# A new plan of work for a decode step: other heads first, fewer second-layer loads, one form of feed-forward

## The chip, the cores and the metric

The kernel runs on one core of a Trainium2 chip. The metric is the time of one execution on the device in microseconds. The core has a matrix engine (PE; its weight loads are shown as PEld), a vector engine (DVE), a scalar engine (ACT), GpSimd (POOL), a queue that issues transfers (SP), and 16 DMA engines that carry them. The engines run side by side, each through its own list of instructions in order, and wait for one another by semaphores.

## The reference

Four tokens (B = 4), one position each, go through attention, feed-forward, attention, feed-forward. The two attentions use the same weights and the same caches, and so do the two feed-forwards.

```python
x = A_x
x = x + _A_ref(_layernorm(x), A_k_cache, A_v_cache, A_wq, A_wo)
x = x + _B_ref(_layernorm(x), B_w_gate, B_w_up, B_w_down)
x = x + _A_ref(_layernorm(x), A_k_cache, A_v_cache, A_wq, A_wo)
x = x + _B_ref(_layernorm(x), B_w_gate, B_w_up, B_w_down)
```

`_A_ref` has 16 query heads on 8 key-value heads of 256 numbers each, and reads the last 2048 of 8192 cache positions: softmax of q.k / 16, times v, times `wo`. `_B_ref` is `(silu(x @ w_gate) * (x @ w_up)) @ w_down` with 1792 inner columns. x has 448 numbers for each token, and all is in bfloat16.

For each token and key-value head there is 1 MiB of keys and 1 MiB of values: 64 MiB for 32 pairs of token and head. The weights are small beside it.

## The kernel before, in words

**Heads and groups.** A unit of work is a head, written as three digits: token, layer (0 first, 1 second), key-value head. PLAN lists the stages in order; in a stage a blank separates groups, "+" joins two heads that share one group (one softmax for both), and "&" does the same with the score matmuls issued for each head apart (or, behind a single head, with the wide form of the scores). `group` (L859) makes the steps of one group: query spread over the array (`qe`, POOL), scores (`sc`, PE, L920), maximum, `spread`, `negm`, `exp`, `turn`, copy (`pt`), sum, the product with the values (`pv`, PE, L1001), and `oh`, `oho`, `flip`, `oT`, which lead to a column for the output projection `out_proj` (L1039). The keys of a half load are first transposed in place on DVE (L887), at one instruction for each half.

**Half loads and slots.** Keys and values are held in SBUF in slots of 512 KiB, one half load each: four for a head. NPOOL = 31 slots are in the pool. NLATE = 7 more lie where the query weights `wq` are, and can be used only after the last query projection. Keys named in WHOLE come as one transfer of two neighbouring slots, the others as two transfers. SLOTS gives the slot of each such transfer in the order of SP's list. A transfer into a slot that is taken waits for the last reader of what lay there: the score matmuls of a key, the `pv` of a value.

**Held halves.** A token's second layer reads the same caches as its first. What HOLD names (a key head counts as two halves, a value half as one) stays in its slot from the first layer to the second. What it does not name is loaded again: 128 half loads for the first layer, and 128 less the held ones for the second.

**The change of layer.** When all eight first-layer heads of a token are done, the stage loop (from L1068) appends: `rows` (the projections added up in row form are split, turned and added), the last output projection in column form (`opc`), `residual`, `norm`, the feed-forward, `norm` again and `qproj`, which gives the query of the second layer. Only after that can the scores of this token's second layer run, and give back what it holds. The feed-forward has two forms: `ffn_row` (L658) for the tokens in ROWF, with the token's hidden values in rows, after which `rows` and `residual` are run again, and `ffn` (L711), with them in columns, which adds straight into x. A token whose second layer is done waits, and its last feed-forward is run together with another token's.

**Order.** `Graph` collects the steps with what each reads and writes, and numbers them as they are made. The order on each engine is not found by the program: SEQ_PE, SEQ_DVE, SEQ_ACT, SEQ_POOL and SEQ_SP are written out, each a list of step numbers. SEQ_PE also has fillers, "w" and a number: a matmul of 512 columns on zeros into bank A (L1137 in the trace, and L543 where one follows another), which only keeps PE at work. The number says behind which reader of bank A it may run. Since SP issues in order, a transfer that waits for its slot holds back all later ones.

```python
if held[s] is not None:
    o.deps[last[id(held[s])]] = True
elif s >= NPOOL:
    o.deps.update((d, True) for d in late)
held[s] = cell
```

These lines of `schedule` give a transfer its slot and its wait.

**Lines.** L521 loads weights (`load`); L875 and L881 load keys, whole and by halves; L897 values; L740 and L776 are the two products of the column feed-forward, L678 and L706 those of the row form; L615 is the query projection; L654 copies the finished query; L812 adds the residual; L820 stores the result.

Of the kernel before, what the change touches and what calls it, by code (L numbers as in the profile page):

```python
# [37 lines left out]
ROWF = (1, 2)  # L38
PLAN = (
# [4 lines left out]
)  # L44
HOLD = (
# [3 lines left out]
)  # L49
WHOLE = (  # L50
    "000 001 002 003 004 005 006 007 010 011 012 014 015 017 100 101 102 103 104 106 107 110 112 202 203 204 206 "
    "211 215 216 300 301 302 303 304 307 314"
)
SEQ_PE = (
# [32 lines left out]
)  # L87
SEQ_DVE = (
# [256 lines left out]
def build(nc, A_x, A_k_cache, A_v_cache, A_wq, A_wo, B_x, B_w_gate, B_w_up, B_w_down, out):  # L345
# [3 lines left out]
    with ExitStack() as es:  # L349
# [718 lines left out]
        for si, (heads, splits) in enumerate(zip(plan(), plan_splits())):  # L1068
# [40 lines left out]
            for t, layer in full:  # L1109
                residual(t)  # L1110
                norm(t, xr)
                if layer == 0:
                    with_, waiting = waiting, []
                    if t in ROWF:
                        ffn_row(with_ + [t])
# [86 lines left out]
```

## Time and profile before

| what | value |
|---|---|
| median of three runs | 277.8 us (275.09, 281.72, 277.8) |
| span of the profiled execution | 277.7 us, from its first to its last instruction; this is the time to which the sums below refer |
| PE busy | 242.4 us, of which the fillers (L1137 and L543) 53.3 and 51.8 |
| DVE busy | 185.0 us |
| ACT and POOL busy | 62.8 and 80.4 us |
| bytes read | 100.77 MB |
| value transfers | 83 of 512 KiB |
| key transfers | 30 of 1024 KiB, 26 of 512 KiB |
| mean TensorE clock granted | 0.984 |

In the rows by stretches of time, each engine's busy time is given with its number of instructions in brackets; the three numbers at the end are the granted clock of PE, the busy share of the DMA engines, and GB/s. In rows in order of time, the first number is the start, the second the duration, then engine, line, operation, result and operands; what the engine waited for stands in square brackets. In rows by group, the busy time and the mean in ns come first, then the idle time of the engine ahead of the group and what ended it. The chain line gives shares of the span along the chain of work that ended last.

### The profile page before, as it was taken

Reading aid. Unit: us, or ns where it says so; the run is one execution under the profiler, and the core shown is the slowest. Engines: PE = TensorE matmul, PEld = TensorE weight load, DVE = VectorE, ACT = ScalarE, POOL = GpSimd, SP = SyncE. Lnnn points to the kernel's source line nnn. Section 1 sums busy time; section 2 is a strip of 40 time slices with the busy share of each in tenths; the row PEclk is TensorE's granted clock in tenths of the full one; section 3 lists DMA queues with packets and bytes.
Section 4 is the critical chain, followed back from the end, with each engine's and each line's share of the span. In section 5 each row is a group of like instructions: output and inputs, shape, how many; then the busy total and the mean of one; then the engine's idle time right before and its main releaser. Section 6 shows DMA issues by size and latency. Waiting matters only on the chain.

```text
span 277.7 us, 10576 instructions
## 1 busy us (share of the span) xinstructions
PE 242.4 (87%) x4751; PEld 126.5 (46%) x4576; DVE 185.0 (67%) x574; ACT 62.8 (23%) x173; POOL 80.4 (29%) x224
## 2 busy tenths in 40 slices
PE   3997999999999887998888887979799787989995
PEld 0121232233475553544445444535455456667664
DVE  4666817735612687978857599986768757389841
ACT  0003021111112222331332333224132321232411
POOL 1160121111024221615044243133234332254350
PEclk9998899999999999999999999999989999999998
DMA  7999999999999999999999999999999998799200
GB/s 278 425 420 413 415 395 418 399 401 406 405 387 417 411 412 414 410 409 411 351 394 400 414 417 411 408 413 408 358 384 350 411 378 297 279 396 411 81 2 3
DMA packets 25740, 101.44 MB, mean 365 GB/s; under 512 B 2523, under 2 KB 6623, under 8 KB 21471
## 3 DMA queue, kind: packets, MB, share of 16 engines
q1 hardware_dynamic: 25687, 100.78, 91.8%
q8 instruction: 36, 0.59, 0.9%
q14 instruction: 9, 0.07, 0.1%
q10 hardware_dynamic: 8, 0.00, 0.0%
HBM read 100.77 MB, written 0.00 MB: 363 GB/s over the span
## 4 chain that ended last, share of the span: by engine, by line
PE 40%; DMA 36%; DVE 14%; issue 3%; ACT 2%; SPq 2%; POOL 2%; DVEq 0%; ACTq 0%
DMA half<-in_A_v_cache_dram 24%; DMA half<-in_A_k_cache_dram 12%; DVE half L887 8%; PE S L920 8%; PE A L543 6%; PE Y L1001 6%; PE A L1137 5%; PE Z L740 3%; PE A L1055 2%; PE Z L776 2%; PE A L1047 1%; PE Y L969 1%; SPq L521 1%; DVE oh L1019 1%; SPq L897 1%
## 5 line engine op out<-in xcount | busy, mean ns | idle before, releaser
L887 DVE STREAM_TRANSPOSE half<-half 128x1024 uint32<-128x1024 uint32 x86 | 104.7, 1229 | 8.8 <-DMA half<-in_A_k_cache_dram 8.8
L1137 PE MATMUL A<-identb,small 128*128 128x512 bf16 x139 | 53.3, 389 | 3.3 <-DVE A L447 2.9
L1015 POOL TENSOR_TENSOR small<-small 128x2 f32<-128x2 f32 (+1 forms) x48 | 38.5, 805 | 47.1 <-DVE small L992 29.7
L543 PE MATMUL A<-identb,small 128*128 128x512 bf16 x175 | 51.8, 397 | 0.0
L920 PE MATMUL S<-half,qe 128*8 128x128 bf16 (+1 forms) x1520 | 45.0, 240 | 6.6 <-issue 2.8
L1001 PE MATMUL Y<-half,pT 128*8 128x256 bf16 (+1 forms) x1024 | 42.9, 274 | 8.4 <-DMA half<-in_A_v_cache_dram 5.0
L920 PEld LDWEIGHTS S<-half,qe 128*8 128x8 bf16 x1520 | 30.5, 84 | 22.3 <-DVE half L887 9.8
L954 ACT ACTIVATE praw<-S,small 104x128 bf16<-104x128 f32 (+2 forms) x48 | 19.4, 404 | 68.3 <-DVE small L950 64.1
L1019 DVE SCALAR_TENSOR_TENSOR oh<-oh,small,Y 128x256 bf16<-128x256 bf16 x48 | 22.5, 468 | 16.9 <-ACT oh L1017 16.7
L926 POOL TENSOR_TENSOR qe<-qc,tiny 128x64 bf16<-128x64 bf16 x64 | 18.1, 294 | 43.9 <-PE S L920 35.2
L1001 PEld LDWEIGHTS Y<-half,pT 128*8 128x8 bf16 (+1 forms) x1024 | 20.2, 84 | 23.0 <-DVE small L992 6.5
L1017 ACT ACTIVATE oh<-Y 128x256 bf16<-128x256 f32 x48 | 18.4, 383 | 45.8 <-PE Y L1001 37.3
L1137 PEld LDWEIGHTS A<-identb,small 128*128 128x128 bf16 x139 | 14.6, 105 | 14.9 <-issue 8.9
L577 POOL TENSOR_SCALAR st<-st 128x1 f32<-128x1 f32 x16 | 4.3, 267 | 57.6 <-DVE st L567 56.4
L978 ACT ACTIVATE pT<-Y 128x64 bf16<-128x64 f32 (+1 forms) x48 | 12.4, 258 | 36.0 <-PE Y L969 29.6
L1055 PE MATMUL A<-wo_sb,oT 128*4 128x448 bf16 x192 | 17.5, 356 | 2.0 <-issue 1.1
L1082 POOL MEMSET oT<- 128x16 bf16 x39 | 4.1, 112 | 38.4 <-PE A L1055 32.1
L992 DVE TENSOR_REDUCE small<-Y 128x2 f32<-128x32 f32 (+1 forms) x48 | 9.1, 189 | 8.8 <-PE Y L986 7.9
L1035 DVE TENSOR_TENSOR oT<-Y,small 128x4 bf16<-128x4 f32 (+1 forms) x63 | 9.0, 155 | 5.8 <-PE Y L1025 4.5
L950 DVE TENSOR_REDUCE small<-S 104x1 f32<-104x32 f32 (+1 forms) x48 | 8.5, 177 | 5.2 <-PE S L944 5.0
L941 PE MATMUL S<-small,identb 104*104 104x32 bf16 (+1 forms) x48 | 10.0, 208 | 1.9 <-DVE tiny L936 1.5
L1025 PEld LDWEIGHTS Y<-tiny,oh 128*128 128x128 bf16 x96 | 7.0, 98 | 9.6 <-DVE oh L1019 4.9
(139 smaller groups left out, 266.9 us busy)
## 6 DMA issues: line engine op xcount, KB each, us to landing
half<-in_A_v_cache_dram SPq DMA_DIRECT2D x83, 512.0 KB, 9.9
half<-in_A_k_cache_dram SPq DMA_DIRECT2D x30, 1024.0 KB, 11.2
half<-in_A_k_cache_dram SPq DMA_DIRECT2D x26, 512.0 KB, 8.9
wo_sb<-in_A_wo_dram SPq DMA_DIRECT2D x8, 448.0 KB, 17.2
half<-in_A_wq_dram SPq DMA_DIRECT2D x3, 1024.0 KB, 8.5
wd_sb<-in_B_w_down_dram SPq DMA_DIRECT2D x1, 1568.0 KB, 18.3
wg_sb<-in_B_w_gate_dram SPq DMA_DIRECT2D x1, 1344.0 KB, 18.0
wu_sb<-in_B_w_up_dram SPq DMA_DIRECT2D x1, 1344.0 KB, 20.8
```

The source lines that it names most:

```text
L543: return e.add_instruction(mybir.InstMatmult(start_tensor_calc=start, stop_tensor_calc=stop, ldweights=load, name=nc.get_next_instruction_ ...
L887: return e.transpose(a, a)
L920: last = e.matmul(Sb[s_][qd:qd + 8, 0:32 * 2 * J], lhsT=qe[q_][:, P, ce, :, :].rearrange("p a n -> p (a n)"), rhs=keys(kcs[P], J * x, J, c ...
L926: g.op(POOL, "qe", lambda e, P=P, t=t, kvh=kvh: e.tensor_tensor(qe[q_][:, P, :, :, :], qc[t][:, kvh, :, :].unsqueeze(2).broadcast_to([128, ...
L954: return e.activation(praw[0:R, 0:N].rearrange("p (g r l) -> p g r l", g=J, l=2), Sb[s_][0:R, 0:N].rearrange("p (l g r) -> p g r l", l=2, ...
L978: g.op(SCA, f"pt{n}", lambda e: e.activation(pf, Yb[p_][:, 0:PW], ACT.Copy), r=(f"yp{p_}",), w=(f"pT{pt}",), bank=(f"Y{p_}",))
L1001: last = e.matmul(Yb[p_][32 * gg:32 * gg + M, 256:512], lhsT=pT[pt][:, gg, 2 * a + hv, 4 * P:4 * P + M] if n == 2 else pf[:, 16 * gg + 8 * ...
L1015: g.op(POOL, f"pow{n}", lambda e: e.tensor_tensor(ri[p_][:, 0:2 * n], rs[p_][:, 0:2 * n], expo[:, 1:1 + 2 * n], op=ALU.pow), r=(f"rs{p_}", ...
L1017: g.op(SCA, "oh", lambda e: e.activation(oh[:, :], Yb[p_][:, 256:512], ACT.Copy), r=(f"y{p_}",), w=("oh",), bank=(f"Y{p_}",))
L1019: g.op(DVE, "oho", lambda e: e.scalar_tensor_tensor(out=oh[:, :], in0=oh[:, :], scalar=lomask[:, 0:1], in1=Yb[p_][:, 256:512], op0=ALU.mul ...
L1055: last = e.matmul(Ab[32 * k:32 * k + B, 0:D], lhsT=oT[oi][:, k % 2, k // 2, :], rhs=wo_sb[:, 4 * kvh + k, :], start=False, stop=False, ski ...
L1137: return e.matmul(Ab[:, 0:512], lhsT=w, rhs=rhs, start=False, stop=False, skip_group_check=True)
```

## The change

All is in the constants; no function is edited. ROWF is empty, so that every feed-forward takes the column form. PLAN has 41 stages instead of 38, and 53 groups instead of 48. In each token's first layer, the heads whose keys and values are not held come first. HOLD names 95 half loads instead of 87, so 33 are loaded again for the second layer instead of 41. WHOLE names other heads. The orders on all five engines and the slots are new; SEQ_PE has 326 fillers instead of 314. The slots 31 to 37 (wq's place) are no longer used. In SP's order the first query weights come later, and the second-layer loads are for the most part behind the last first-layer loads.

```diff
-ROWF = (1, 2)
+ROWF = ()
 PLAN = (
-    "005+001", "002+000", "006", "007", "003+004", "101 102", "100", "017+015", "016&014", "107 013", "103 105",
-    "106", "104", "010", "202", "201", "200 012", "113&114", "117+204", "203 115", "116 205", "206 207", "011 302",
-    "110", "305 300", "213+216", "214&301", "303", "215+217", "304", "306+307", "112", "211 212&111", "313+316",
-    "314+317", "210&310", "311&", "315&312",
+    "002", "000+005", "004", "006+001", "003& 007", "101 100&", "017", "014", "013&012", "010", "015&", "103& 105",
+    "104& 102&", "106 107", "016 201", "200", "115 114", "117+113", "207&", "116&206", "204&", "203", "202&", "205",
+    "112 301", "300", "011", "213", "216", "217 215", "214+212", "305& 306&", "303+302", "304", "307", "110&",
+    "210", "211&", "111", "314+316", "313+312", "315+317", "310+311",
 )
 HOLD = (
-    "k03 k04 k05 k06 k07 k13 k14 k15 k16 k17 k21 k23 k24 k25 k26 k27 k31 k33 k34 k36 k37 v001 v021 v030 v031 v040 "
...
+    "k00 v000 v001 k02 v020 v021 k03 v031 k04 v040 v041 k05 v050 v051 k06 v060 k07 v070 v071 k12 v120 k13 v130 v131 "
+    "k14 v140 v141 k15 v150 v151 k16 v160 v161 k17 v170 v171 k22 v220 v221 k23 v230 v231 k24 v240 v241 k25 v250 v251 "
+    "k26 v260 v261 k27 v270 v271 k32 v320 v321 k33 v330 v331 k34 v340 v341 k35 v350 v351 k36 v360 v361 k37"
 )
...
 SEQ_SP = (
-    "119 47 48 49 128 124 50 51 154 189 159 158 157 162 123 127 122 213 235 150 192 151 163 242 237 322 193 216 "
...
+    "152 118 148 47 178 49 233 207 335 48 202 50 51 143 237 358 121 234 182 140 122 210 147 151 146 240 174 200 282 "
...
 SLOTS = (
-    "0 2 5 13 18 26 7 15 20 28 4 3 10 12 25 23 8 5 17 16 13 14 2 26 15 4 20 5 6 26 27 20 22 29 21 6 26 20 0 5 22 "
...
-    "28 5 17 18 24 25 5 10 4 31 32 33 34 35 36 37 28 25"
+    "28 8 11 2 4 15 22 17 20 6 13 24 30 0 14 25 27 19 26 10 4 15 16 1 29 0 16 19 15 7 6 16 19 15 7 4 2 9 20 17 10 0 "
+    "12 11 15 30 14 13 29 8 27 25 13 22 28 26 24 25 27 23 13 22 24 27 2 20 4 16 0 11 7 10 15 29 14 8 19 30 9 18 12 17 "
+    "27 11 6 17 12 11 27 28 6 12 11 2 24 22 3 5 20 1 16 15 26 8 0 19 13 14 30 29 17 18 9 10 13 29 17 7 9 18 13 7 14 "
+    "25 3 17 24 7 4"
 )
```

More of the change, by code (lines that the diff above doesn't have):

```diff
@@ L30 @@
 FAR = 1e30
-ROWF = (1, 2)
+ROWF = ()
 PLAN = (
[4 rows of a table removed]
[4 rows of a table added]
 )
 HOLD = (
[3 rows of a table removed]
[3 rows of a table added]
 )
 WHOLE = (
-    "000 001 002 003 004 005 006 007 010 011 012 014 015 017 100 101 102 103 104 106 107 110 112 202 203 204 206 "
-    "211 215 216 300 301 302 303 304 307 314"
+    "000 001 002 003 004 005 006 007 011 100 101 102 103 104 105 106 110 111 200 202 203 204 205 206 300 301 302 304 "
+    "306 307 310 311"
 )
 SEQ_PE = (
[32 rows of a table removed]
[32 rows of a table added]
 )
 SEQ_DVE = (
[22 rows of a table removed]
[21 rows of a table added]
 )
 SEQ_ACT = (
[8 rows of a table removed]
[8 rows of a table added]
 )
 SEQ_POOL = (
[9 rows of a table removed]
[9 rows of a table added]
 )
 SEQ_SP = (
[7 rows of a table removed]
[6 rows of a table added]
 )
 SLOTS = (
[4 rows of a table removed]
[4 rows of a table added]
 )
```

156 rows, old and new, of tables (HOLD, SEQ_ACT, SEQ_DVE, SEQ_PE) are left out of this document.

## The prediction

> **What bounds the kernel now.** I read the page first, then the DMA rate by stretches of time, then the order of matmuls at the places where a token changes layer, and last the queue SP at the stretches where the rate falls.
>
> ```profile
> span 277.7 us, 10576 instructions
> HBM read 100.77 MB, written 0.00 MB: 363 GB/s over the span
> DMA half<-in_A_v_cache_dram 24%; DMA half<-in_A_k_cache_dram 12%; DVE half L887 8%; PE S L920 8%; PE A L543 6%; PE Y L1001 6%; PE A L1137 5%; PE Z L740 3%; PE A L1055 2%; PE Z L776 2%; PE A L1047 1%; PE Y L969 1%; SPq L521 1%; DVE oh L1019 1%; SPq L897 1%
> ...
> core 0: us, PE busy (x) PEld busy (x) DVE busy (x) ACT busy (x) POOL busy (x), PEclk, DMA share, GB/s
> 5.00:135.00 130.00, 119.08 (x1902) 49.81 (x1755) 80.92 (x239) 23.56 (x65) 31.68 (x84) 0.99 1.03 409
> 135.00:140.00 5.00, 4.41 (x91) 2.29 (x84) 4.00 (x17) 1.41 (x4) 0.40 (x2) 1.00 0.89 329
> 140.00:195.00 55.00, 46.51 (x1089) 26.89 (x1080) 43.31 (x122) 17.69 (x50) 19.61 (x56) 1.00 1.02 408
> 195.00:215.00 20.00, 18.24 (x401) 10.72 (x385) 14.99 (x42) 4.44 (x12) 6.34 (x18) 0.91 0.99 363
> 215.00:225.00 10.00, 7.96 (x180) 4.31 (x179) 7.18 (x20) 2.90 (x8) 4.49 (x12) 1.00 1.02 413
> 225.00:240.00 15.00, 12.38 (x333) 9.54 (x328) 8.85 (x35) 2.26 (x9) 2.58 (x11) 1.00 0.80 295
> 240.00:245.00 5.00, 4.57 (x85) 2.23 (x84) 2.12 (x9) 2.62 (x5) 2.42 (x8) 1.00 0.99 356
> 259.00:278.00 19.00, 14.66 (x370) 10.86 (x363) 7.65 (x39) 3.89 (x10) 6.25 (x14) 0.93 0.02 6
> ```
>
> The chain of waits is led by loads of keys and values. The last column of the stretches says how: 409 GB/s without a break to 135 us, and almost nothing after 259. So the time is the stream of loads at 409 GB/s, plus the dips, plus the 18.7 us of arithmetic behind the last landing. Each dip is worth (409 minus its rate) times its length over 409: 1.0 us at 135, 2.25 us at 195, 4.2 us at 225 and 0.65 us at 240, 8.1 us in all. 3.25 us of that lies ahead of 223 us.
>
> The Trainium skill, page "DMA: Bandwidth & Descriptors", section "Where 436 GB/s comes from", says that HBM holds a core to about 358 GB/s; the 409 over 130 us disagrees, and the measurement decides (by the page the saved bytes below would be worth 11.7 us).
>
> A dip comes where a load waits for a buffer slot. The longest such wait is a token's change of layer: its last first-layer value lands, its last head, output projection, norm, feed-forward, norm and query projection follow in series, and only then do the scores of its second layer give slots back. Token 0, then token 3 and the end:
>
> ```profile
> 68.78 0.61 PE L1001 MATMUL Y<-half,pT 128*8 128x256 bf16 x16 [0.19 <-DMA half<-in_A_v_cache_dram]
> 76.50 1.46 PE L740 MATMUL Z<-xn,wg_sb 128*128 128x32 bf16 x42
> 82.94 1.89 PE L776 MATMUL Z<-wide,wd_sb 128*128 128x32 bf16 x56
> 91.30 1.11 PE L920 MATMUL S<-half,qe 128*8 128x256 bf16 x32 [0.47 <-POOL oT L1082]
> ...
> 223.73 1.05 PE L1001 MATMUL Y<-half,pT 128*8 128x256 bf16 x32
> 245.24 1.11 PE L920 MATMUL S<-half,qe 128*8 128x256 bf16 x32
> 264.20 1.05 PE L1001 MATMUL Y<-half,pT 128*8 128x256 bf16 x32
> 275.36 0.85 SPq L820 DMA_DIRECT2D out_dram<-wo_sb  x1
> ```
>
> From the last value's product to the first second-layer score, token 0 takes 22.5 us and token 3 takes 21.5 us. From token 3's product (223.73) to the end of the span it is 54.0 us.
>
> **The change, part by part.**
>
> *Loads.* HOLD keeps 95 half loads instead of 87 (26, 23, 24 and 22 for tokens 0 to 3; before 22, 20, 22 and 23), so 8 of 0.524 MB go, 4.19 MB: 10.25 us at 409 GB/s. Counted along SP's order, 84.1 MiB end with token 3's last first-layer value before and 80.1 MiB after, so all of it is saved ahead of that point.
>
> *Where it is given back.* 31 slots carry everything, since the seven in wq's place are no longer used. More held means fewer that rotate: while token 0 changes layer the SLOTS list shows five (16, 19, 15, 7, 6). I counted in SP's order how much is loaded between a token's last first-layer value and the first load that needs a slot from its second layer, at 2.56 us per MiB. Before: 30.5, 29.4, 28.2 and, for token 3, 19.2 us. After: 19.9, 21.8, 20.5 and 23.0 us. The cover needed is the change of layer, a score, and the time until a refilled queue streams again:
>
> ```profile
> 73.68 0.65 PE L920 MATMUL S<-half,qe 128*8 128x128 bf16 x32
> ...
> 229.53 1.20 SPq L897 DMA_DIRECT2D half<-in_A_v_cache_dram  x2
> ...
> 228.00:228.50 0.50, 0.50 (x26) 0.48 (x26) 0.50 (x1) 0.00 (x0) 0.00 (x0) 1.00 0.65 262
> 229.50:230.00 0.50, 0.17 (x6) 0.16 (x9) 0.32 (x3) 0.00 (x0) 0.00 (x0) 1.00 0.18 74
> 230.50:231.00 0.50, 0.50 (x18) 0.38 (x16) 0.50 (x1) 0.00 (x0) 0.42 (x2) 1.00 1.02 393
> ...
> 11.02 1.24 PE L543 MATMUL A<-identb,small 128*128 128x512 bf16 x5
> ```
>
> A single head's score is 0.65 us. After the issue at 229.53 the rate is back at 230.5, and it had sunk since 228.0: a drained queue costs 1 us behind the issue and 1 ahead, I take 2. With token 3's 19.2 us of cover, its 21.5 us less the 3 us that its slots do not wait for, and 2, the old order would lose 1.3 us; the dip there was 4.85, so such sums are rather low. The new order on PE is thinner inside the changes: 13, 10, 4 and 6 fillers instead of 37, 20, 13 and 10, and 11, 21, 24 and 20 other steps of attention instead of 18, 32, 30 and 23. A filler in a row takes 1.24/5 = 0.25 us, so token 0 could lose 24 x 0.25 = 6 us of its 22.5, or nothing where the filler only stood in a wait. I take half: 19.5 us, and the same for tokens 1 and 2. Then 19.5 + 0.65 + 2 = 22.2 us is needed, and the stalls are 2.3, 0.4 and 1.7 us, 4.4 us (with 22.5 us they are 13.4, with 16.5 none).
>
> Beside these, loads with a cover of only 2.0 to 2.5 MiB (5 to 6.4 us) wait for single scores and value products: 20 ahead of token 3's last value, before 9. The 9 cost the two dips of 3.25 us; 20 would cost 7.2 us at that price, but a stall at one gives the next its slack, so I add 2.1 us to the chain stalls (bounds 0 and 7.2). Together 6.5 us against 3.25: 3.25 us given back.
>
> *Start.* wq's last part comes at 10.4 instead of 6.0 MiB, 11 us later, so scores begin near 40 us, not 29.26. The first load that needs a slot is at 20.6 MiB, some 53 us; it waits for the fourth group's score, and three groups at about 3 us fit ahead of it. Nothing, at worst 3 us.
>
> *Column feed-forward for tokens 1 and 2.*
>
> ```profile
> 73.97 0.16 DVE L812 TENSOR_TENSOR xr<-xr,A 128x4 f32<-128x4 f32 x1
> 90.33 0.29 DVE L654 CAST qc<-Z 128x128 bf16<-128x128 f32 x1 [0.40 <-PE Z L543]
> 127.17 0.16 DVE L812 TENSOR_TENSOR xr<-xr,A 128x4 f32<-128x4 f32 x1 [0.29 <-PE A L1047]
> 143.88 0.29 DVE L654 CAST qc<-Z 128x128 bf16<-128x128 f32 x1
> ```
>
> Residual to query takes 16.4 us in the column form (token 0) and 16.7 in the row form (token 1): nothing, between -1.5 and +1.5.
>
> *DVE.*
>
> ```profile
> L887 DVE STREAM_TRANSPOSE half<-half 128x1024 uint32<-128x1024 uint32 x86 | 104.7, 1229 | 8.8 <-DMA half<-in_A_k_cache_dram 8.8
> L1019 DVE SCALAR_TENSOR_TENSOR oh<-oh,small,Y 128x256 bf16<-128x256 bf16 x48 | 22.5, 468 | 16.9 <-ACT oh L1017 16.7
> L992 DVE TENSOR_REDUCE small<-Y 128x2 f32<-128x32 f32 (+1 forms) x48 | 9.1, 189 | 8.8 <-PE Y L986 7.9
> L950 DVE TENSOR_REDUCE small<-S 104x1 f32<-104x32 f32 (+1 forms) x48 | 8.5, 177 | 5.2 <-PE S L944 5.0
> ```
>
> 78 transposes, not 86, save 8 x 1.23 = 9.8 us; 53 groups, not 48, add 5 x (0.47 + 0.19 + 0.18 and some 0.4 for the maximum and the scaling) = 6 us. All of it lies under a stream at which DVE is 62% busy (80.92 of 130 us), so it counts as nothing; without that cover it would be -4 us.
>
> *End.* Behind token 3's value four pairs of heads and three single ones follow, about as before, but the change of layer holds four fillers and three steps fewer: 1 + 1 us off the 54.0. The late second-layer loads do not set it: 12 MiB, 30.7 us, lie behind that value, and the last lands some 20 us ahead of the end.
>
> *Sum*, from the profiled 277.7 (the median shown is 277.8, the three runs 275.09 to 281.72): 277.7 - 10.25 + 3.25 - 2 = 268.7 us, 3.2% faster.
>
> **The rivals.** *The gain is eaten at the changes of layer.* The fillers only stood in waits, and the changes still take 22.5 us: stalls of 13.4 + 2.1 instead of 3.25, and nothing off the end: 279.7. For it: the dip at token 3 was larger than my sum. Halfway it is 274. A second road to it is the clock:
>
> ```profile
> 196.90 1.05 PE L920 MATMUL S<-half,qe 128*8 128x256 bf16 x16
> 199.86 1.54 PE L920 MATMUL S<-half,qe 128*8 128x256 bf16 x16 [0.88 <-DVE half L887]
> 202.00:203.00 1.00, 1.00 (x21) 0.28 (x9) 0.00 (x0) 0.37 (x2) 0.28 (x2) 0.50 1.02 373
> ```
>
> After some 2 us of little work on PE the clock granted is 0.50, and the same score takes 1.54, not 1.05 us. The 0.91 over the 20 us from 195 is some 3.6 us at half speed, and 3.6 x (1 - 1.05/1.54) = 1.15 us lost. 33 fillers instead of 80 inside the changes make that likelier; once in each of four, it costs 4.6 us: 273.3. The Trainium skill, page "TensorE: Matmul & The Clock Gate" (its advice on idle gaps), puts the danger at gaps over about 3 us; by that the thinner order loses nothing, while the trace shows it after shorter ones.
>
> *Slower: five slots cannot rotate fast enough.* Five slots are 6.4 us of stream, eight and seven (tokens 1 and 2) 10.2 and 9.0. If load, use and reissue take 14 us, the rate in some 20 us of each change falls by 54%, 27% and 36%: 23 us, against the 3.25 of now, and the time is 287. It turns slower by 2% from about 12.5 us on. For it: a value lands 9.9 us after its issue in the median of the page. Against: that is time in a full queue, which a starved one does not have.
>
> *Faster still.* The new changes take 16.5 us, only the short covers cost, about as now, and the end gains 2 to 5 us: 262 to 265.
>
> *It does not do what it says:* excluded, the lists themselves count 161 half loads instead of 169.
>
> **How the numbers follow.** Forecast (265 to 273.5) 0.42; gain eaten (273.5 to 283.4) 0.29; faster still 0.15; slower 0.14. A measurement of this kernel tells 2% from no change, 272.2 and 283.4 us. Under 272.2 lie the faster case and most of the forecast, 0.53; between the two the rest of it and nearly all of the eaten gain, 0.33; slower 0.14. The range 261 to 281 leaves out 0.04 below and about 0.16 above.
>
> **What would show it.** HBM read near 96.6 MB, the transposes 78 times. The rate holds near 409 to about 85 us and dips where tokens change layer; the dips ahead of token 3's last value sum to 6.5 us. Token 0 takes 19.5 us from value to score, token 3's last product runs near 217 us, and 52 us follow. If the dips sum to over 12 us the first rival holds; if long stretches run at half the rate, the slots. I am wrong if the rate is whole and the time is not shorter: then arithmetic binds.

## The result, and the profile after

The change makes the kernel slower: 294.6 us in the median against 278.3, ratio 1.059 with a 95% interval of 1.049 to 1.069. The prediction was 268.7 us. Here and below, medians are of all executions, and ratios leave out the slower, disturbed ones, so that the two differ a little for some rows.

The page of the changed kernel first (the profiled execution took 295.5 us, its span is 293.7). Below the busy times stand the rows of granted clock and GB/s in 40 slices, and the chain that ended last.

```profile
span 293.7 us, 11005 instructions
...
PE 270.2 (92%) x4983; PEld 133.8 (46%) x4751; DVE 178.1 (61%) x582; ACT 65.0 (22%) x186; POOL 81.1 (28%) x220
...
PEclk9999999999877999985999999758999795998577
...
GB/s 299 417 427 415 417 400 397 376 245 384 395 401 204 326 419 412 407 393 170 327 395 403 410 392 286 387 279 278 345 419 359 400 326 249 404 312 360 7 2 3
...
q8 instruction: 38, 0.62, 0.8%
...
HBM read 96.57 MB, written 0.00 MB: 329 GB/s over the span
...
PE 84%; DVE 8%; issue 5%; ACT 2%; POOL 0%; POOLq 0%
```

The same rows of the kernel before:

```profile
PE 242.4 (87%) x4751; PEld 126.5 (46%) x4576; DVE 185.0 (67%) x574; ACT 62.8 (23%) x173; POOL 80.4 (29%) x224
...
PE 40%; DMA 36%; DVE 14%; issue 3%; ACT 2%; SPq 2%; POOL 2%; DVEq 0%; ACTq 0%
```

The bytes are gone as foreseen (96.57 MB). But loads have left the chain of work that ended last: PE has 84% of it. PE is busy for 27.8 us more, in a span that is 16.0 us longer, so it is idle for 11.8 us less. (Busy times of PE rest on modelled ends of matmuls.) By stretches of time, with the granted clock, the busy share of DMA and GB/s at the end of each row:

```profile
core 0: us, PE busy (x) PEld busy (x) DVE busy (x) ACT busy (x) POOL busy (x), PEclk, DMA share, GB/s
55.00:70.00 15.00, 14.78 (x214) 4.46 (x181) 6.83 (x19) 2.57 (x9) 3.70 (x6) 1.00 0.82 302
70.00:85.00 15.00, 13.54 (x259) 8.38 (x249) 4.89 (x27) 3.23 (x10) 2.29 (x7) 0.78 1.04 400
85.00:100.00 15.00, 13.83 (x254) 7.50 (x248) 4.96 (x20) 2.88 (x7) 4.29 (x13) 0.88 0.78 264
130.00:150.00 20.00, 19.36 (x419) 12.50 (x407) 11.94 (x41) 4.79 (x14) 3.43 (x13) 0.76 0.78 284
175.00:210.00 35.00, 32.81 (x751) 19.82 (x746) 22.15 (x78) 9.87 (x30) 11.38 (x34) 0.80 0.87 309
```

The rate dips at the start and at each change of layer. By the prediction's formula the rows from 55, 85, 130 and 175 us are worth 3.9, 5.3, 6.1 and 8.6 us, 24 us ahead of token 3's last first-layer value, where 6.5 were expected. The clock, 0.895 in the mean (0.984 before), is low around the changes of layer, not at the start; at token 0 it falls ahead of the dip (0.78 from 70 to 85 us, at 400 GB/s).

Where a token changes layer, in order of time on PE (start, duration, line): token 0's last first-layer value product and its first second-layer score, and token 3's last value product.

```profile
74.93 0.39 PE L999 MATMUL Y<-half,pT 128*4 128x256 bf16 x8
...
95.56 0.34 PE L918 MATMUL S<-half,qe 128*8 128x128 bf16 x12
...
239.74 0.61 PE L999 MATMUL Y<-half,pT 128*4 128x256 bf16 x16
```

The change of layer itself is not longer: 20.6 us for token 0 (22.5 before). Behind token 3's product come 54.0 us, just as before; that product itself is 16.0 us later, at 239.74 instead of 223.73.

Two kinds of rows name what is new. The waits of PE that nothing in the profile releases ("issue"; us in total, times, longest), first after, with the shortest three left out, then before:

```profile
PE S L918 <- issue: 2.4, 5, 0.7
PE A L1045 <- issue: 2.0, 1, 2.0
PE Y L984 <- issue: 1.5, 1, 1.5
PE A L1053 <- issue: 1.4, 1, 1.4
PE Y L1023 <- issue: 1.3, 1, 1.3
...
```

```profile
PE S L920 <- issue: 2.8, 2, 1.7
PE A L1055 <- issue: 1.1, 1, 1.1
PE Y L1001 <- issue: 0.9, 2, 0.6
```

With the three left out, that is 10.1 us in 12 pieces against 4.8 in five. And the runs of fillers, here on PE after, ahead of the score of token 0's head 7 at 64.56 us:

```profile
59.93 4.70 PE L541 MATMUL A<-identb,small 128*128 128x512 bf16 x21
```

### The profile page after: what moved, and what is told of

It reads as the page before. It is cut to its first block, busy times and chain, and to the rows that moved or that the text cites. A ratio compares the mean times of both kernels' runs of the same rounds, so it can differ in the third digit from the quotient of the medians.

```text
span 293.7 us, 11005 instructions
## 1 busy us (share of the span) xinstructions
PE 270.2 (92%) x4983; PEld 133.8 (46%) x4751; DVE 178.1 (61%) x582; ACT 65.0 (22%) x186; POOL 81.1 (28%) x220
## 3 DMA queue, kind: packets, MB, share of 16 engines
HBM read 96.57 MB, written 0.00 MB: 329 GB/s over the span
## 4 chain that ended last, share of the span: by engine, by line
PE 84%; DVE 8%; issue 5%; ACT 2%; POOL 0%; POOLq 0%
PE A L541 15%; PE Y L999 14%; PE S L918 14%; PE A L1135 8%; PE Z L738 6%; PE A L1053 5%; PE Z L613 4%; PE Y L967 3%; DVE half L885 3%; PE Z L774 3%; PE S L939 2%; PE Z L559 2%; PE Y L1023 2%; PE Y L984 2%; PE A L1045 2%
## 5 line engine op out<-in xcount | busy, mean ns | idle before, releaser
L885 DVE STREAM_TRANSPOSE half<-half 128x1024 uint32<-128x1024 uint32 x78 | 94.8, 1226 | 10.5 <-DMA half<-in_A_k_cache_dram 10.4
L541 PE MATMUL A<-identb,small 128*128 128x512 bf16 x232 | 61.4, 394 | 0.2 <-DVE xr L810 0.2
L999 PE MATMUL Y<-half,pT 128*4 128x256 bf16 (+1 forms) x1024 | 53.2, 298 | 0.7 <-issue 0.3
L918 PE MATMUL S<-half,qe 128*8 128x128 bf16 (+1 forms) x1488 | 48.7, 247 | 3.0 <-issue 2.4
L1135 PE MATMUL A<-identb,small 128*128 128x512 bf16 x94 | 38.2, 408 | 3.1 <-DVE A L445 2.7
L1015 ACT ACTIVATE oh<-Y 128x256 bf16<-128x256 f32 x53 | 20.2, 381 | 66.7 <-PE Y L999 44.9
L952 ACT ACTIVATE praw<-S,small 104x128 bf16<-104x128 f32 (+2 forms) x53 | 21.8, 412 | 48.0 <-DVE small L948 46.2
L999 PEld LDWEIGHTS Y<-half,pT 128*4 128x4 bf16 (+1 forms) x1024 | 19.9, 86 | 14.6 <-DVE small L990 5.1
L1135 PEld LDWEIGHTS A<-identb,small 128*128 128x128 bf16 x94 | 10.1, 107 | 10.4 <-issue 5.9
L939 PEld LDWEIGHTS S<-small,identb 104*104 104x104 bf16 (+1 forms) x53 | 6.2, 117 | 18.7 <-DVE tiny L934 9.5
L934 DVE TENSOR_REDUCE tiny<-S 104x1 bf16<-104x128 f32 (+2 forms) x27 | 8.9, 328 | 7.4 <-PE S L918 7.3
L1023 PE MATMUL Y<-tiny,oh 128*128 128x2 bf16 (+1 forms) x106 | 10.8, 170 | 2.5 <-issue 1.3
## 6 DMA issues: line engine op xcount, KB each, us to landing
wo_sb<-in_A_wo_dram SPq DMA_DIRECT2D x8, 448.0 KB, 14.1
```

The costliest lines, as they stand in the source:

```text
L541: return e.add_instruction(mybir.InstMatmult(start_tensor_calc=start, stop_tensor_calc=stop, ldweights=load, name=nc.get_next_instruction_ ...
L885: return e.transpose(a, a)
L918: last = e.matmul(Sb[s_][qd:qd + 8, 0:32 * 2 * J], lhsT=qe[q_][:, P, ce, :, :].rearrange("p a n -> p (a n)"), rhs=keys(kcs[P], J * x, J, c ...
L952: return e.activation(praw[0:R, 0:N].rearrange("p (g r l) -> p g r l", g=J, l=2), Sb[s_][0:R, 0:N].rearrange("p (l g r) -> p g r l", l=2, ...
L999: last = e.matmul(Yb[p_][32 * gg:32 * gg + M, 256:512], lhsT=pT[pt][:, gg, 2 * a + hv, 4 * P:4 * P + M] if n == 2 else pf[:, 16 * gg + 8 * ...
L1015: g.op(SCA, "oh", lambda e: e.activation(oh[:, :], Yb[p_][:, 256:512], ACT.Copy), r=(f"y{p_}",), w=("oh",), bank=(f"Y{p_}",))
```

## The experiments

"before" and "after" are the two kernels. Ratios are to the kernel before, measured beside it; a difference in us is a difference of ratios times 277.8.

| run | what is done | median, us | ratio [95%] |
|---|---|---|---|
| after | | 294.6 | 1.059 [1.049, 1.069] |
| b_half | before, refilling loads halved | 267.5 | 0.965 [0.960, 0.970] |
| a_half | after, the same | 274.6 | 0.987 [0.982, 0.993] |
| b_less | before, 4.19 MB less | 273.7 | 0.988 [0.984, 0.992] |
| a_no22 | after, one run of fillers out | 288.3 | 1.036 [1.030, 1.042] |
| a_start | after, prologue of before | 291.1 | 1.042 [1.036, 1.048] |
| a_s22 | after, both, transposes in the order of the keys' landing | 290.5 | none |
| a_greedy | after, slots dealt anew | 299.3 | 1.082 [1.075, 1.089] |
| a_unhold | the same, eight halves not held | 301.4 | 1.091 [1.084, 1.098] |
| a_row | after, row feed-forward | 301.5 | 1.081 [1.073, 1.089] |
| b_col | before, column feed-forward | 285.8 | 1.029 [1.020, 1.038] |
| a_thick | after, 49 fillers more | 300.8 | 1.072 [1.060, 1.083] |
| a_few | after, 98 fillers fewer | 289.6 | 1.034 [1.028, 1.040] |
| b_few | before, 112 fillers fewer | 281.7 | 1.018 [1.012, 1.025] |
| b_thin | before, 47 fewer in the changes | 279.5 | 1.005 [1.000, 1.010] |
| b_dim | before, 112 made small matmuls | 294.6 | 1.063 [1.056, 1.069] |
| a_pvhalf | after, half of the value products | 288.6 | 1.043 [1.032, 1.054] |
| b_pvhalf | before, the same | 279.7 | 1.002 [0.997, 1.007] |
| a_l1 | after, second-layer loads halved | 286.4 | 1.032 [1.025, 1.038] |

### Is the stream the limit? b_half, a_half, b_less

```diff
-unit(cell), vsrc[hv]
+unit(cell)[:, 0:g.part(cell)], vsrc[hv][:, 0:g.part(cell)]    # part: HALF // 2, HALF at a slot's first use
```

Keys are cut in the same way, so parts of the attention are left out. The first load into each slot stays whole, so that the stream is lighter only behind the first fill of the slots. In b_less only 16 value halves are cut.

> The kernel before with every key and value load after the first use of a slot cut to half its columns (the other half of the slot keeps older data, so the output is not the reference's); all orders, slots and arithmetic stay. It shows how long the order takes when the stream of loads is not the limit: some 130 half loads at 0.26 MB less are 34 MB, 83 us of stream. Theory A (the stream and its slots set the time of both kernels): 225 to 250 us. Theory B (arithmetic in its written order sets the time): over 265 us.

> The changed kernel with the same cut (output not the reference's). Theory A (the changed kernel is longer because its stream stops for slots): it falls by 40 us or more and is no longer than the kernel before with the same cut, within 3 us. Theory B (its order of arithmetic itself is longer): it stays 8 us or more above the kernel before with the same cut.

> The kernel before with 16 of its half loads of values, spread evenly ahead of token 3's last first-layer value, cut to half their columns (the rest of the slot keeps older data, so the output is not the reference's): 4.19 MB less, as the change saves, and nothing else moved. The prediction's first term (bytes at 409 GB/s, all of it on the path): 10 us less, a ratio of 0.964. Theory B (arithmetic in its order is only a few us behind the stream, as the run with all loads halved gained 10.7 us for 36 MB): 1 to 3 us less.

With 36 MB less the kernel before gains only 9.8 us (3.5% of 277.8). It reads at 409 GB/s, yet its arithmetic, in its order, is only about 10 us behind. 4.19 MB are worth 1.2% (0.8 to 1.6), 3.4 us, a little above theory B's 1 to 3 and not 10.25. The halved changed kernel stays 6 us above the halved kernel before (0.987 less 0.965), between what theory A (3) and theory B (8) allowed; and it falls by 20 us, half of what theory A asked for. So both have a part. Their token residuals (tokens 0 and 3, added on DVE) show where; a_half first, then b_half, then the two full kernels:

```profile
79.72 0.16 DVE L816 TENSOR_TENSOR xr<-xr,A 128x4 f32<-128x4 f32 x1 [0.65 <-PE Y L996]
228.24 0.12 DVE L816 TENSOR_TENSOR xr<-xr,A 128x4 f32<-128x4 f32 x1
...
PE A L1057 <- issue: 0.7, 1, 0.7
```

```profile
71.48 0.16 DVE L818 TENSOR_TENSOR xr<-xr,A 128x4 f32<-128x4 f32 x1
218.89 0.16 DVE L818 TENSOR_TENSOR xr<-xr,A 128x4 f32<-128x4 f32 x1
```

```profile
78.84 0.16 DVE L810 TENSOR_TENSOR xr<-xr,A 128x4 f32<-128x4 f32 x1 [0.67 <-PE Y L984]
242.92 0.12 DVE L810 TENSOR_TENSOR xr<-xr,A 128x4 f32<-128x4 f32 x1
```

```profile
228.57 0.16 DVE L812 TENSOR_TENSOR xr<-xr,A 128x4 f32<-128x4 f32 x1
```

| stretch, us | before | after | b_half | a_half |
|---|---|---|---|---|
| to token 0's residual | 74.0 | 78.8 | 71.5 | 79.7 |
| from there to token 3's | 154.6 | 164.1 | 147.4 | 148.5 |
| from there to the end | 49.1 | 50.8 | 46.4 | 44.8 |

These are single executions. Up to token 0's residual the changed order is 4.9 us later with the full loads and 8.2 with the halved ones, which up to there still run at 362 GB/s in a_half and 394 in b_half; so the loss there is not the price of the stream. Between the residuals the two orders differ by 1.1 us beside the lighter stream and by 9.5 beside the full one: the full stream costs the changed order 15.6 us there, and the kernel before 7.2. PE's busy time in this stretch shows what the 15.6 are; before, b_half, after, a_half:

```profile
73.97:228.57 154.60, 134.74 (x2981) 77.55 (x2934) 111.43 (x318) 41.91 (x120) 50.15 (x139) 0.99 1.01 399
71.48:218.89 147.41, 132.74 (x2974) 77.09 (x2927) 110.99 (x318) 41.69 (x120) 50.01 (x139) 1.00 0.65 219
78.84:242.92 164.08, 152.27 (x3197) 87.87 (x3152) 108.89 (x325) 43.04 (x129) 51.09 (x135) 0.88 0.93 352
79.72:228.24 148.52, 144.57 (x3197) 85.48 (x3152) 108.61 (x326) 43.05 (x129) 51.07 (x135) 0.93 0.61 201
```

Beside the lighter stream the changed order (53 groups instead of 48, in 43 stages, not the 41 given above) keeps PE busy for 11.8 us longer than the old one, though it runs fewer fillers there (98 instead of 119). Nearly all of it goes into waits that PE had anyway: its idle time falls from 14.7 to 4.0 us. Beside the full stream the same 3197 matmuls are busy for 7.7 us longer, at a clock of 0.88 instead of 0.93, and PE is idle for 7.9 us longer. PE's unexplained waits are of that size: 0.7 us in the whole of a_half, all of it outside this stretch, and 10.1 after, 8.1 of it inside. In the kernel before the full stream lengthens the busy time by 2.0 us and the idle time by 5.2.

### The start: a_no22, a_start, a_s22

```diff
-w1 w1 w1 w1 w1 w1 w1 w1 w1 w1 w1 w1 w1 w1 w1 w1 w1 w1 w1 w1 w1 w1 265 193
+265 193
```

265 is the score of head 7. a_start has wq and the norms in SP's, PE's and DVE's lists as in before:

```diff
-152 118 148 47 178 49 233 207 335 48 202 50 51 143
+118 47 48 49 148 178 50 51 152 233 207 335 202 143
```

> The changed kernel without the run of 22 fillers (4.9 us from 59.7 us on) that stands on PE ahead of the score of token 0's head 7. Theory A1 (that run delays the value products that slots wait for, and with them the loads): token 0's residual comes 4 to 5 us earlier, the rate does not dip at 60 to 65 us, and the time falls by 3 to 5 us. Rival (PE waited there for the keys of head 7 in any case): within 1 us of the changed kernel.

> The changed kernel with the prologue of the kernel before: the parts of wq right behind the first key load, the steps of the norms and the first query projection on PE and DVE in the order of before with its fillers, and 26 fillers fewer at the first two score groups. Behind that nothing is moved. Theory S (the late start costs the difference that the two halved runs show up to token 0's residual, 8 us, and nothing covers it): first query at 27 to 28 us instead of 35.6, token 0's residual 5 to 8 us earlier, and 286 to 290 us. The prediction's view (a late start costs nothing, at worst 3 us): 291 to 296.

> The changed kernel with the earlier prologue of the run a_start, transposes on DVE in the order in which their keys land, and without the 22 fillers ahead of the score of head 7. If the two losses at the start are separate (6.4 us by the fillers alone, 3.5 us by the prologue alone) they sum to 10 us: 284 to 286. If both are the same wait: 287 to 290.

The 22 fillers alone are worth 6.4 us (1.059 to 1.036). But theory A1 does not hold: without them PE waits 2.72 us at the same score for transposed keys, and token 0's residual comes only 1 us earlier (77.87), token 3's 5.7 us (237.18). Most of the gain arises behind the place that was changed; from token 0's residual to token 3's the clock is 0.92 there, not 0.88, and what links the two is not shown. a_start is some 4.7 us faster than the changed kernel, and the intervals just part. It has 86 fillers fewer, which may be part of that. It has its first query at 26.68 us, nine earlier, and yet token 0's residual at 81.51 in its profile (of an execution of 293.1 us): from 45 to 50 us DVE is busy for all 5 us, mostly with transposes, in a list made for later scores, and PE for 0.39. So it does not show what an early query is worth, and where its gain arises is open. a_s22, with 284.4 to 291.5 us, settles nothing.

### Slots and held halves: a_greedy, a_unhold

```diff
 HOLD = (
-    ... v000 v001 ... v050 v051 ... v160 v161 ... v240 v241 ...
+    ... (these eight left out; their loads are put into SEQ_SP)
```

> The changed kernel with its 31 slots dealt out anew: each load takes the slot that comes free earliest in PE's order; loads, their order and all engines stay. It is the control of the next run. If the slots' assignment mattered, up to 4 us less; otherwise within 2 us of 294.6.

> The changed kernel with the hold of eight value halves undone (four of token 0, two each of tokens 1 and 2), so that 169 half loads are made as before and that many more slots rotate; slots dealt out by the same rule as in the run before. Theory H (too few rotating slots at the changes of layer stop the stream, and that is the loss behind token 0's residual): 4 to 10 us less than the run before, although 4.19 MB more are loaded. The prediction's price (10.25 us for those bytes, 3.25 us of stalls given back): 7 us more. Neither (arithmetic and its order): within 2 us.

In a_unhold eight half loads are made again, so its steps are numbered anew. Dealing the slots by the simple rule costs 6 us by itself, so which slot a load gets matters, and the written list is better than that rule. Against that control, eight halves fewer held is not faster; the intervals overlap. More slots do mend the rate where it dips; around token 0's change of layer, first a_greedy, then a_unhold:

```profile
85.00:100.00 15.00, 13.60 (x252) 7.05 (x246) 5.60 (x22) 2.88 (x7) 4.31 (x13) 0.89 0.61 204
85.00:100.00 15.00, 13.72 (x249) 7.17 (x239) 5.50 (x22) 2.88 (x7) 4.31 (x13) 0.89 0.88 317
```

From 130 to 150 us it is 224 against 282 GB/s. So theory H falls: the rate comes back and the time does not. The 4.19 MB more cost some 2.5 us, not clear of noise, against the prediction's 7.

### The form of the feed-forward: a_row, b_col

```diff
-ROWF = (1, 2)
+ROWF = ()
```

That is b_col; a_row is the reverse. The steps of the new form stand where those of the old one stood.

> The changed kernel with the row form of the feed-forward for tokens 1 and 2 put back, at the same places in the orders. Prediction's step (column form costs 0, between -1.5 and +1.5 for both): within 2 us. Rival (its small matmuls keep the clock low and cost time): 3 us or more less.

> The kernel before with the column form of the feed-forward for tokens 1 and 2, at the places of the row form. The prediction's step: within 1.5 us for both tokens. As the row form made the changed kernel 6 us longer, the column form could gain 3 to 6 us here; more work on PE could cost 2 us.

Each is slower than its own kernel: the row form in the changed kernel by 6.2 us, the column form in the kernel before by 8.0 (5.5 to 10.4). So a swap of the form is not free, and what it costs depends on the order around it: in b_col PE has an unexplained wait of 2.42 us inside the feed-forward's products of token 2, and the clock is at half from 183 to 197 us (0.51). Putting one form into an order planned for the other does not price the form in its own order; that stays open.

### Fillers and the clock: a_thick, a_few, b_few, b_thin, b_dim

```diff
-w1 w1 w1 195 w1 136 w1 w1 w1 w1 w1 w1 138
+w1 195 w1 136 w1 138        # a_few, b_few; in b_dim those left out become 7 matmuls of 32 columns each
```

b_thin takes 47 out and a_thick puts 49 in, between a token's last first-layer value and its first second-layer score.

> The changed kernel with 49 fillers more inside the changes of layer of tokens 0, 1 and 2 (24, 10 and 15), so that they count about as in the kernel before. Theory C (the clock that falls to half there is what costs the time): mean granted clock 0.95 or more instead of 0.895 and 5 to 10 us less. Rival (clock not the cost, or the fillers stand on the path): clock may rise, the time is the same within 2 us or up to 6 us longer.

> The changed kernel with every row of fillers behind the first scores cut to a single one (98 fillers fewer, 24 us of PE at full clock). Theory F (PE, 92% busy, is held up by fillers that stand ahead of due steps): 8 to 15 us less. Theory C (fillers hold the clock up and cost nothing): the mean granted clock falls under 0.85 and the time rises by 3 us or more.

> The kernel before with the same cut. Theory F: 0 to 5 us less (its fillers stand in waits for the stream). Theory C: the clock falls as in the changed kernel, to about 0.9, and the time rises by 3 to 10 us; then the fillers are what the change lost.

> The kernel before with 47 fillers fewer, all inside the four changes of layer, which leaves 13, 10, 4 and 6 as the changed kernel has. The prediction's step (half of their time comes off the changes): 2 to 6 us less. Its rival (the clock falls for it): the clock at half in the changes of layer, mean under 0.95, and 2 to 6 us more. Neither: within 2 us, clock 0.97 or more; then the missing fillers alone are not what lets the clock fall in the changed kernel.

> The kernel before with the 112 fillers that stand behind another filler (behind the first groups) each replaced by seven matmuls of 32 columns, which take as long on PE (7 x 35 ns) but are the sort under which the clock stayed at half during the feed-forward. Theory K (the clock by itself costs): mean granted clock under 0.93 and 5 us or more longer. If the clock falls and the time stays within 2 us, the clock by itself costs nothing; if the clock stays at 0.98, the run says nothing on it.

The mean granted clocks of before, after, b_thin and b_few are 0.984, 0.895, 0.956 and 0.917, in spans of 277.7, 293.7, 277.9 and 279.6 us. If a low clock is always the half one, these are 8.9, 61.7, 24 and 46 us at half speed (twice what is missing from 1, times the span). b_thin shows that fillers missing in the changes do let the clock close (0.53 from 72 to 83 us), and that this costs 1.4 us (0 to 2.9). b_few has 37 us more at half speed for 5 us (3.4 to 6.8), with 112 fillers less to run. In the changed kernel fewer fillers are faster, not slower: 98 out give 7 us (1.059 to 1.034), and in the executions of 287.2 and 285.9 us the clock is 0.91 and 0.92, no lower than with them. With 49 more it is 0.94 and 0.96 in those of 299.5 and 295.3 us, and nothing is gained. So in this order these fillers cost more by their place in PE's list than they earn by the clock, and theory C, by which fillers cost nothing, falls for the changed kernel; in the kernel before, where PE has waits to fill, they earn their place. That does not make the low clock free. b_dim is 17 us longer, but it does not price the clock: beside its 784 small matmuls the unexplained waits are 14.1 us, not 4.8 (one of 2.04 us within a group of scores).

### PE's own work: a_pvhalf, b_pvhalf

```diff
-Yb[p_][32 * gg:32 * gg + M, 256:512]
+Yb[p_][32 * gg:32 * gg + M, 256:384]    # and the values' columns alike
```

> The changed kernel with the value products over half of their columns (128 of 256 in each; half of the attention output stays zero, so the output is not the reference's). It takes up to some 20 us of work off PE and leaves loads, slots and orders. Theory P (PE is the limit of the changed kernel): 10 us or more less. Theory L (latencies and waits for slots set it): under 5 us less.

> The kernel before with the same cut. Theory P: its stream and PE are both near the limit, so 2 to 6 us less, at any rate less than in the changed kernel. Theory L: as in the changed kernel.

In the kernel before, half of the value products makes no difference. In the changed kernel it gives about 4.6 us, though the two intervals overlap. That points to PE as the limit of the one and not of the other, but the 10 us that theory P asked for are not there.

### The late second-layer loads: a_l1

```diff
+if layer == 0:
+    g.first |= {id(c) for c in kc}    # these stay whole; the second layer's are halved
```

> The changed kernel with only its 33 second-layer half loads cut to half their columns (the rest of the slot keeps older data, so the output is not the reference's): 8.65 MB less, nearly all of it late. The prediction's step (the late loads do not set the end; 52 us follow token 3's value): the time from token 3's residual to the end stays near 51 us and the total falls by under 3 us. Rival (late loads hold up the end, by slots, or by the stalls of PE's instruction stream that come only beside a full stream): that stretch falls to 45 us and the total by 5 to 9 us.

```profile
238.70:283.60 44.90, 39.72 (x1017) 27.77 (x1015) 27.64 (x112) 11.90 (x33) 16.23 (x44) 0.88 0.32 101
...
242.92:293.70 50.78, 44.46 (x1017) 29.31 (x1015) 27.60 (x112) 11.93 (x33) 16.21 (x44) 0.77 0.49 189
```

These rows run from token 3's residual to the end, a_l1 first, then the changed kernel: 44.9 us, not 50.8, and the kernel is 7.5 us faster (1.059 to 1.032). The late loads do hold up the end, as the rival said, but not by waits for them, of which PE has none here: 4.7 of the 5.9 us are the same 1017 matmuls busy for longer, at a clock of 0.77 instead of 0.88, and 1.2 are unexplained waits (2.0 instead of 0.8).

## Why the prediction was wrong

What PE waited for longest in the kernel before (total, times, longest) has no like in the changed one:

```profile
PE Y L1001 <- DMA half<-in_A_v_cache_dram: 5.0, 8, 1.0
```

- **"So the time is the stream of loads at 409 GB/s, plus the dips".** This is the step that failed. 409 GB/s without a break is true, but a full stream is not a sole limit: b_half shows arithmetic some 10 us behind it. The term "all of it is saved" measures 3.4 us (b_less), not 10.25. A gain of 3% was not to be had from these bytes. And the sum has no term for PE's own list: between the residuals the new order keeps PE busy for 11.8 us longer (a_half against b_half). The prediction's last line, that arithmetic binds if the time is not shorter, is what came; only its condition, a whole rate, did not.
- **Stalls at the changes of layer.** 6.5 us were forecast, and the dips sum to 24. But to read them as the loss was wrong: in the changed kernel no load is among what PE waits for (in the kernel before values lead that list, 5.0 us in eight waits), the change itself takes 20.6 us (19.5 forecast), and a_unhold mends the rate without gaining time. So the rate most likely falls because PE's list, and with it the release of slots, is late: every wait of SP ahead of a load of keys or values is for a step of PE. The sign given for the first rival, dips over 12 us, did not tell the two apart.
- **Start: "Nothing, at worst 3 us".** 4.9 us measured up to token 0's residual, and 8.2 in the halved pair. The three groups in front of the first slot wait were counted at 3 us each, without the 21 fillers of 4.70 us among them; yet a_no22 gets only 1 us back there without them, so what makes the start late stays open.
- **Column feed-forward, 0 within 1.5.** By its own measure it held: residual to query takes 15.1 and 17.5 us for tokens 1 and 2 in the changed kernel, 32.6 in all, and 16.7 and 16.0 before, 32.7. But that interval is not the whole price, since b_col, with the form swapped in the old order, is 8.0 us longer. The two tokens in the changed kernel:

```profile
134.37 0.16 DVE L810 TENSOR_TENSOR xr<-xr,A 128x4 f32<-128x4 f32 x1 [1.06 <-PE A L541]
149.47 0.29 DVE L652 CAST qc<-Z 128x128 bf16<-128x128 f32 x1 [0.36 <-PE Z L541]
...
186.98 0.16 DVE L810 TENSOR_TENSOR xr<-xr,A 128x4 f32<-128x4 f32 x1 [0.65 <-PE A L1045]
204.47 0.29 DVE L652 CAST qc<-Z 128x128 bf16<-128x128 f32 x1 [0.38 <-PE Z L541]
```

- **DVE, nothing.** Right: 61% busy, and 8% of the chain.
- **End, -2.** Measured 0: 54.0 us both times, counted from token 3's product (from its residual it is 1.7 longer). "The late second-layer loads do not set it" was wrong; a_l1 takes 5.9 us off the stretch behind token 3's residual.
- **The second road of the first rival, the clock.** Its mechanism was right: b_thin shows the clock closing for want of fillers. Four times 1.15 us was its price; b_thin has 1.4 us in all. In the changed kernel the clock is at half for 53 us more than before, which it did not foresee. At b_few's rate (5 us for 37) that would be some 7 us. But where PE has no waits left the price is higher: against a_half the same matmuls of the changed kernel are busy for 7.7 us longer with some 19 us more at half speed, against a_l1 at the end for 4.7 with some 13, so about 0.4 us for each, if the clock is all that lengthens them. By that the 53 us would be worth some 20. Both are estimates from these runs, and neither is settled.
- **The slower rival, five slots.** The time came out on its side, but a_unhold speaks against its mechanism.

What is shown: of the 16.0 us of span, 4.9 are lost up to token 0's residual, 9.5 between the residuals and 1.7 behind. Of the 9.5, 1.1 are there beside the lighter stream too. The other 8.4 are what the full stream costs this order more than the old one: 5.7 in PE's busy time (7.7 against 2.0) and 2.7 in its idle time (7.9 against 5.2), which in the changed kernel is unexplained waits and in the kernel before for the most part waits for loads and other engines. That the 5.7 are the lower clock fits, but stays open: no run held the clock up without adding to PE's list. Why a full stream should go with a lower clock and with those waits is not shown either.

## What to carry to other kernels

A queue that never rests shows that something is limiting, not that it is the only limit: halve its bytes once, and see how far the time falls, before bytes are traded against anything else. When a planned order fills every wait of an engine with work, delays elsewhere no longer disappear in those waits. A dip in the rate where slots run short may be the trace of a late releaser, and is then no loss of its own: here the dip could be filled without gain.

## What the runs showed of the hardware

**PE stops without a shown cause beside a full stream of loads.** In the changed kernel, a group of four matmuls of one step is cut in two, by a wait that no semaphore explains:

```profile
127.09 0.35 PE L1053 MATMUL A<-wo_sb,oT 128*4 128x448 bf16 x1
128.83 0.36 PE L1053 MATMUL A<-wo_sb,oT 128*4 128x448 bf16 x3 [1.40 <-issue]
```

Such waits sum to 10.1 us beside the full loads (329 GB/s over the span), and to 0.7 us in a_half (229 GB/s) with the same 11005 instructions. The page lists a queue that carries instructions, 38 packets with 0.62 MB, 16 KB each. That these packets wait among the loads fits, but no run shows it directly.

**The clock can close after about 1 us of little work, and stays closed over a feed-forward.** Granted clock is the third number from the end, in the changed kernel at token 0's change of layer and at token 1's:

```profile
76.00:77.00 1.00, 0.04 (x2) 0.04 (x4) 0.31 (x1) 0.91 (x3) 0.00 (x0) 1.00 1.02 402
77.00:78.00 1.00, 0.80 (x22) 0.61 (x22) 0.94 (x5) 0.22 (x1) 0.00 (x0) 1.00 1.00 375
78.00:80.00 2.00, 1.80 (x37) 1.37 (x33) 0.77 (x8) 0.47 (x1) 0.00 (x0) 0.58 1.07 378
80.00:84.00 4.00, 4.00 (x116) 3.78 (x116) 0.82 (x5) 0.50 (x2) 1.60 (x6) 0.50 1.08 404
128.00:129.00 1.00, 0.17 (x3) 0.09 (x3) 0.00 (x0) 0.00 (x0) 0.00 (x0) 1.00 1.03 414
130.00:140.00 10.00, 9.50 (x194) 6.07 (x185) 7.09 (x19) 1.34 (x5) 1.92 (x7) 0.51 0.58 214
```

PE is busy for all of 80 to 84 us, and the clock stays at half: the work there is matmuls of 32 columns. They lose nothing by it. 42 of them take 1.47 us here and 1.46 in the kernel before at full clock:

```profile
80.77 1.47 PE L738 MATMUL Z<-xn,wg_sb 128*128 128x32 bf16 x42
```

Not every such gap closes it. In the kernel before, PE is as idle from 109 to 110 us, and the clock stays at 1.00 behind it; what parts the two cases is not shown:

```profile
109.00:110.00 1.00, 0.20 (x6) 0.10 (x5) 0.00 (x0) 0.00 (x0) 0.00 (x0) 1.00 0.97 401
110.00:112.00 2.00, 2.00 (x41) 0.97 (x34) 1.88 (x4) 0.48 (x2) 0.85 (x3) 1.00 1.02 412
```

The Trainium skill, page "TensorE: Matmul & The Clock Gate", section "HAM oscillation — how this bites in real kernels", puts the danger at idle gaps over some 3.4 us; by its later section "A second HAM failure mode: psum-queue depth-cycling", frequent short idling between groups is enough. The first does not bound it here, since the clock fell behind gaps of 0.99 and 1.40 us; the second is nearer, though here a single such gap went before each fall.
